# Attention, experts and a dense network on one core: buffers for keys and values, and the load and scatter times of the order

## The chip, the cores and the metric

The kernel runs on one core of a Trainium2 chip. The metric is the device time of one execution in microseconds (us), the median of several executions; smaller is better. Five engines work side by side, each in the order of its own instruction list: PE (TensorE, matrix products; its weight loads are a row of their own, PEld), DVE (VectorE), ACT (ScalarE), POOL (GpSimd) and SP (SyncE, which here only issues transfers and reads registers).

## The reference

Three stages follow one another on float32 data:

```python
def sm_attn(qq, kk, vv):
    s = scale * np.matmul(qq, kk.transpose(0, 1, 3, 2))
    s = s - np.max(s, axis=-1, keepdims=True)
    a = np.exp(s)
    a = a / (np.sum(a, axis=-1, keepdims=True) + 1e-09)
    return np.matmul(a, vv)
p_packed = sm_attn(p, k, v)          # 32 queries per head over 576 keys
out = sm_attn(q, p_packed, p_packed) # 576 queries per head over 32 keys
```

q, k and v are 8 x 8 x 576 x 64 (batch, head, position, width), p is 8 x 8 x 32 x 64. The output, as 4608 tokens of width 512, goes to a mixture of 8 experts: each token goes to the one expert with the largest logit (`x @ w_gate` plus a bias by modality), which computes `gate * (relu(x @ w1[e]) @ w2[e])` with a hidden width of 1024. The last stage is a dense network, `g(x @ w_in) @ w_out` with `g(h) = h * sigmoid(1.702 h)` and a hidden width of 2048; its weights come as float64.

## The kernel before

The attention works in eight units: a unit is a pair of batches and one half of the heads (4), and two units make a pair of batches complete. `loads` (lines 236 to 250) brings in the keys, queries and values of a unit, 1.2 MB each, in two transfers per tensor, which SP issues. `stage1` turns the keys with the identity into the tile kT (L447 on PE, L227 or L228 for the copy out), computes the scores (L293), their maxima and exponentials, turns these (L343), and multiplies them with the values (L366). `qT` turns the queries, and `stage2` computes the second attention: scores (L498), subtraction of the maximum, exponential, sum, a normalization on POOL (L526), its turning (L543) and the products (L564). `store` (L580) writes 1152 KB of tokens to a table xs in memory.

When both units of a pair are done, `route` (L590 ff.) picks each token's expert and its place in that expert's list, and POOL writes the list with nine scatters (`send`, L187), 128 tokens each. Three early slots of an expert's work, then a fourth, begin before the attention has ended: `expert` reads registers, `whole_gather` (L1269 ff.) reads a piece of the list on SP (tok<-lst, L1278) and gathers the tokens with POOL (L1281); L1115 and L1423 are the two products of an expert. Then come the remaining slots, and the dense network by blocks of 512 tokens (L1115 and L1545), behind whose start the 32 weight transfers of L1216 and L1221 are taken apart and split by DVE and ACT.

No engine's order is written by hand. Every piece of work is handed to a planner (`Sched`) with an engine, an assumed duration, the tiles that it writes and reads, and a priority. `run` keeps one clock per engine. Again and again it takes the piece that can start earliest (by priority, where several can), and writes its instructions into the program at that place. A piece can start when its engine is free, when everything that it depends on has ended and a latency has passed, and when a buffer for each of its tiles is free; a tile of n buffers may be made again when the tile n places before has been read by all its readers. The latency behind a load is LAT["sp"], unless the piece names its own; the latency behind one of the nine scatters is SEND, and the list read depends on all scatters of its pair of batches. A piece may also have a due time (`after=`) before which the plan doesn't start it: `expert` gives its register reads the due times 110.0, 150.0, 189.9 and 229.9 us of the plan's clock (T - 30000 ns). These numbers make the order only; on the chip each instruction starts when its engine reaches it and what it waits for is done. The chip's waits follow the order in which the program was written: a list read waits for all scatters written before it, and a scatter written behind a list read waits for that read.

The planned duration of an attention load on SP is 3500 ns, of a scatter on POOL 1270 ns, of one register read 550 ns, of an expert's weight load 1500 ns. The loads of the dense network's weights name their own latency (2200).

Of the kernel before, what the change touches and what calls it, by code (L numbers as in the profile page):

```python
# [50 lines left out]
class Sched:  # L51

    LAT = {"pe": 250.0, "sp": 2200.0, "pq": 2200.0}

    def __init__(self):
        self.made, self.given, self.held, self.ops = {}, {}, {}, []
# [5 lines left out]
    def add(self, eng, dur, fn, w=(), r=(), hold=(), prio=0.0, lat=None, deps=(), after=0.0, alts=None):  # L64
# [3 lines left out]
        o.alts = alts or {eng: (dur, fn)}  # L68
        o.lat = self.LAT.get(eng, 170.0) if lat is None else lat
        o.deps = list(deps)  # L70
# [122 lines left out]
def attention(tc, ctx, pctx, c, S, ins, xs, lst, early, scatter_key):  # L193
# [7 lines left out]
    q, k, v, p = ins["q"], ins["k"], ins["v"], ins["p"]  # L201
# [4 lines left out]
    def sb(tag, shape, n=2, dtype=F32):  # L206
        def make():
            serial[0] += 1
            return pw.tile(shape, dtype, tag=tag, name=f"{tag}_{serial[0]}", bufs=n)

        return S.buf(tag, make, n)
# [24 lines left out]
    def loads(u, prio):  # L236
        bp, hg = units[u]
        s = st[u]
        hs = slice(4 * hg, 4 * hg + 4)
        for n, src, bufs, by in (("k", k, 1, 0 if u else -1000), ("q", q, 2, 200), ("v", v, 2, 400)):  # L240
            b = s[n] = sb(n, [P, 4, S0], bufs)

            def load(b=b, src=src):
                for bl in range(2):
                    x = src[2 * bp + bl, hs].rearrange("h s d -> h (s d)")
                    nc.sync.dma_start(
                        b.t[:, 2 * bl : 2 * bl + 2],
                        x.rearrange("(g x) (p y) -> (x p) g y", x=2, p=64),
                    )

            S.add("sp", 3500, load, w=[b], prio=prio + by)
# [338 lines left out]
    def route(bp, L, xr, prio):  # L590
# [72 lines left out]
        def send(j):  # L663
            scatter(
                tc,
                scatter_key,
                c,
                lst,
                bass.IndirectOffsetOnAxis(ap=idx.t[:, j : j + 1], axis=0),
                c["ids"][:, bp, j],  # L670
                None,
            )

        for j in range(n):
            c["sends"].append(
                S.add("pool", 1270, lambda j=j: send(j), r=[idx], prio=prio + j, lat=SEND)
            )
# [36 lines left out]
    for u in range(len(units)):  # L714
        loads(u, (u - 2) * CYC)
# [11 lines left out]


CYC = 1000.0
SEND = 4500.0  # L730

WIDE_UNITS = 6

# [1011 lines left out]
```

## Time and profile before

| | |
|---|---|
| median of 3 executions | 1467.85 us (1465.35 to 1472.35) |
| the profiled execution | 1466.42 us |
| its span, from the first to the last instruction | 1464.6 us |
| PE busy | 1389.6 us, 95% |
| DVE, ACT, POOL busy | 727.6, 499.5, 227.8 us |
| mean granted clock of TensorE | 0.976 |
| moved | 142.64 MB, mean 97 GB/s |

The span is that of one execution taken by the hardware profiler. Busy time counts an engine's instructions; in the rows below, what stands in brackets behind an arrow is how long the engine had been idle before the instruction and what ended that. "issue" there means that the engine waited for nothing that the profile shows. L12 is line 12 of the kernel. The granted clock is the share of full speed that TensorE was given. The trace of SP and of POOL's transfers shows when a transfer was issued, not when it landed.

### The profile page before, as it was taken

How to read it: one execution, taken by the hardware profiler on the slowest of the kernel's cores; microseconds unless marked ns; L12 is line 12 of the kernel's file. 1: busy time of each engine (PE TensorE's matmuls, PEld its weight loads, DVE VectorE, ACT ScalarE, POOL GpSimd, SP SyncE). 2: the span in 40 equal slices, each digit the busy share in tenths (PEclk: the TensorE clock that was granted, in tenths of full speed). 3: DMA queues.
4: the chain of work that ended last, by engine and by line, in shares of the span. 5: the costliest groups of instructions: out<-in, count | busy, mean ns of one | idle time of the engine just before them, and what ended most of it. 6: DMA issues, size and time to landing. Idle time of an engine off the chain costs nothing.

```text
span 1464.6 us, 21602 instructions
## 1 busy us (share of the span) xinstructions
PE 1389.6 (95%) x8444; PEld 1154.4 (79%) x8444; DVE 727.6 (50%) x1425; ACT 499.5 (34%) x937; POOL 227.8 (16%) x301
## 2 busy tenths in 40 slices
PE   6886879998999999999989999999999999999997
PEld 5774557887888888888868888888888888888885
DVE  5675545543687878877773332423224242322222
ACT  3554433443344444433232222323223232322221
POOL 0133250410344333100010010100001010010101
PEclk9998889999999999999999999999999999999999
DMA  8866513744466665643131020201002010000000
GB/s 280 249 192 186 175 40 110 160 143 142 142 192 189 190 198 175 203 142 113 64 109 58 3 70 0 72 1 44 29 0 73 0 58 1 0 29 1 30 0 29
DMA packets 128144, 142.64 MB, mean 97 GB/s; under 512 B 29504, under 2 KB 92992, under 8 KB 128032
## 3 DMA queue, kind: packets, MB, share of 16 engines
q1 hardware_dynamic: 113184, 121.86, 27.3%
q0 software_dynamic: 14848, 19.30, 4.5%
q8 instruction: 68, 1.11, 0.3%
q14 instruction: 44, 0.36, 0.1%
HBM read 112.24 MB, written 28.87 MB: 96 GB/s over the span
## 4 chain that ended last, share of the span: by engine, by line
PE 49%; issue 18%; POOL 3%; DVE 2%; DMA 2%; POOLq 0%; ACT 0%; DVEq 0%; SPq 0%; ACTq 0%
PE b_f L1115 25%; PE o L1545 21%; PE o L1423 4%; POOL nat L1348 3%; DMA nat<-xs,si 1%; POOL out L187 0%; DMA raw<-moe_w_in 0%; DVE two L1370 0%; DVE war L1196 0%; DVE wbr L1196 0%; DMA out<-raw,tok 0%; DVE g L1412 0%; DVE xT L1379 0%; DVE raw L1573 0%; DVE t L1246 0%
## 5 line engine op out<-in xcount | busy, mean ns | idle before, releaser
L1115 PE MATMUL b_f<-xT,wac 128*128 128x512 f32 x1404 | 339.6, 391 | 4.5 <-ACT xT L1500 3.6
L1545 PE MATMUL o<-wbc,g 128*128 128x512 f32 x1404 | 337.6, 389 | 1.3 <-DVE raw L1573 0.8
L1115 PEld LDWEIGHTS b_f<-xT,wac 128*128 128x128 f32 x1404 | 265.2, 189 | 60.6 <-ACT xT L1500 4.0
L1115 PE MATMUL b_f<-xT,war 128*128 128x470 f32 (+1 forms) x1284 | 301.3, 383 | 9.0 <-DVEq L1633 6.3
L1545 PEld LDWEIGHTS o<-wbc,g 128*128 128x128 f32 x1404 | 263.3, 188 | 57.0 <-DVE raw L1573 1.2
L1535 DVE SCALAR_TENSOR_TENSOR two<-two,b_f 128x512 f32<-128x512 f32 x144 | 98.9, 687 | 372.8 <-ACT two L1532 372.6
L1115 PEld LDWEIGHTS b_f<-xT,war 128*128 128x128 f32 x1284 | 242.5, 190 | 48.9 <-issue 7.4
L1532 ACT ACTIVATE two<-b_f 128x512 f32<-128x512 f32 x144 | 86.1, 598 | 413.0 <-PE b_f L1115 413.0
L1423 PE MATMUL o<-g,wbr 128*128 128x470 f32 x960 | 222.5, 379 | 1.6 <-DVE g L1412 1.6
L1423 PEld LDWEIGHTS o<-g,wbr 128*128 128x128 f32 x960 | 181.0, 190 | 27.2 <-DVE g L1412 2.4
L187 POOL DMA_INDIRECT out<-raw,tok x36 | 37.7, 1048 | 821.1 <-ACT raw L1575 814.7
L1541 DVE TENSOR_TENSOR g<-two,g 128x512 fp32r<-128x512 f32 x141 | 97.5, 692 | 81.5 <-ACT g L1538 81.1
L1538 ACT CAST g<-two 128x512 fp32r<-128x512 f32 x141 | 87.5, 621 | 112.2 <-DVE two L1535 103.9
L1348 POOL DMA_INDIRECT nat<-xs,si x90 | 93.4, 1038 | 173.8 <-DVE two L1370 94.8
L1409 ACT ACTIVATE g<-b_f 128x470 fp32r<-128x470 f32 x80 | 45.1, 564 | 121.2 <-PE b_f L1115 118.6
L1190 ACT CAST wbr<-raw 128x512 fp32r<-128x512 f32 x80 | 49.6, 620 | 69.2 <-PE o L1423 63.8
L1412 DVE SCALAR_TENSOR_TENSOR g<-b_f,g 128x470 fp32r<-128x470 f32 x80 | 51.4, 643 | 43.2 <-ACT g L1409 43.2
L1545 PE MATMUL o<-wbr,g 128*128 128x512 f32 x288 | 69.5, 390 | 0.0
L1196 DVE TENSOR_TENSOR wbr<-raw,wbr 128x512 fp32r<-128x512 f32 x80 | 55.8, 698 | 21.7 <-ACT wbr L1190 21.5
L1196 DVE TENSOR_TENSOR war<-raw,war 128x512 fp32r<-128x512 f32 x80 | 55.4, 692 | 16.3 <-ACT war L1190 11.6
L1545 PEld LDWEIGHTS o<-wbr,g 128*128 128x128 f32 x288 | 53.9, 188 | 11.9 <-DVE g L1541 0.4
L1190 ACT CAST war<-raw 128x512 fp32r<-128x512 f32 x80 | 49.3, 616 | 20.0 <-DMA raw<-moe_w 17.0
(211 smaller groups left out, 1089.2 us busy)
## 6 DMA issues: line engine op xcount, KB each, us to landing
raw<-moe_w SPq DMA_DIRECT2D x160, 256.0 KB, 3.4
yT<-two SPq DMA_DIRECT2D x40, 235.0 KB, 3.7
k<-k SPq DMA_DIRECT2D x16, 576.0 KB, 5.3
q<-q SPq DMA_DIRECT2D x16, 576.0 KB
v<-v SPq DMA_DIRECT2D x16, 576.0 KB, 9.4
xs<-xr SPq DMA_DIRECT2D x8, 1152.0 KB, 5.9
nat<-yT SPq DMA_DIRECT2D x9, 1024.0 KB
raw<-moe_w_in SPq DMA_DIRECT2D x16, 512.0 KB, 4.5
```

Of the source, the lines that this page charges most:

```text
L1115: nc.tensor.matmul(h.t[:, 0:n], wa[:, a, kc], x[kc].t[:, b, 0:n], start=(kc == 0 and i == 0), stop=(kc == 3 and i == 2),)
L1190: nc.scalar.copy(d, src(i))
L1196: nc.vector.tensor_tensor(d, src(i), h.bitcast(F32), ALU.subtract)
L1348: nc.gpsimd.indirect_dma_start(self.rows(xg)[:, b], None, xs, bass.IndirectOffsetOnAxis(ap=idx.t[:, b : b + 1], axis=0))
L1409: nc.scalar.activation(g.t[:, 0, 0:W], h.t[:, 0:W], AF.Relu)
L1412: nc.vector.scalar_tensor_tensor(g.t[:, 1, 0:W], h.t[:, 0:W], 0.0, g.t[:, 0, 0:W].bitcast(F32), ALU.max, ALU.subtract,)
L1423: nc.tensor.matmul(os[d].t[:, 0:W], w.t[1][:, a, d * P : (d + 1) * P], g.t[:, b, 0:W], start=(fc == 0 and m == 0), stop=(fc == NC1 - 1 and ...
L1532: nc.scalar.activation(th.t, h.t, AF.Tanh, scale=0.851)
L1535: nc.vector.scalar_tensor_tensor(th.t, th.t, 1.0, h.t, ALU.add, ALU.mult)
L1538: nc.scalar.copy(g.t[:, 0], th.t)
L1541: nc.vector.tensor_tensor(g.t[:, 1], th.t, g.t[:, 0].bitcast(F32), ALU.subtract)
L1545: nc.tensor.matmul(os[k].t, g.t[:, a, k * P : (k + 1) * P], w.t[1][:, b], start=(i == 0 and m == 0), stop=(i == n - 1 and m == 2),)
```

## The change

Three numbers that the planner uses are changed, and the numbers of buffers of two tiles are exchanged. No instruction is added or removed. The planner assumes 4500 instead of 2200 ns from the end of a load's issue to the start of its readers (all loads of both plans that don't name a latency of their own: the attention's, the list reads and the experts' weights) and 8000 instead of 4500 ns behind a scatter of the lists. A key tile has two buffers instead of one, and a value tile one instead of two; all are of 9216 bytes per partition, so the memory used is the same.

```diff
-    LAT = {"pe": 250.0, "sp": 2200.0, "pq": 2200.0}
+    LAT = {"pe": 250.0, "sp": 4500.0, "pq": 2200.0}
...
-        for n, src, bufs, by in (("k", k, 1, 0 if u else -1000), ("q", q, 2, 200), ("v", v, 2, 400)):
+        for n, src, bufs, by in (("k", k, 2, 0 if u else -1000), ("q", q, 2, 200), ("v", v, 1, 400)):
...
 CYC = 1000.0
-SEND = 4500.0
+SEND = 8000.0
```

## Rows read from the trace of the kernel before

**Rows 1.** The page: PE's busy time (share) and instructions, and its 40 slices.

```profile
PE 1389.6 (95%) x8444; PEld 1154.4 (79%) x8444; DVE 727.6 (50%) x1425; ACT 499.5 (34%) x937; POOL 227.8 (16%) x301
...
PE   6886879998999999999989999999999999999997
```

**Rows 2.** Table by stage: stretch, its length, busy time (instructions) by engine, granted clock, DMA.

```profile
0.00:280.00 280.00, 229.91 (x3247) 178.19 (x3248) 161.30 (x519) 121.67 (x285) 83.95 (x134) 0.91 0.60 172
280.00:1465.00 1185.00, 1159.64 (x5199) 976.25 (x5197) 566.26 (x906) 377.87 (x652) 143.82 (x168) 0.99 0.26 80
120.00:160.00 40.00, 25.27 (x357) 16.49 (x353) 21.55 (x74) 14.47 (x35) 19.02 (x24) 0.76 0.67 173
160.00:196.00 36.00, 29.80 (x497) 23.94 (x481) 23.50 (x80) 18.89 (x41) 3.59 (x6) 0.93 0.44 138
210.00:220.00 10.00, 9.64 (x58) 5.70 (x59) 2.82 (x9) 4.36 (x12) 8.27 (x7) 0.70 0.19 27
```

**Rows 3.** Waits of PE, 0 to 280 us: total, times, longest.

```profile
PE b L366 <- issue: 12.5, 8, 3.7
PE b L543 <- POOL A L526: 10.2, 2, 5.1
PE b L447 <- DMA k<-k: 8.8, 3, 5.0
```

**Rows 4.** POOL in order of time: start, duration, instruction [idle before].

```profile
133.09 0.97 POOL L187 DMA_INDIRECT lst<-ids,idx  x1 [0.19 <-issue]
...
144.34 0.97 POOL L187 DMA_INDIRECT lst<-ids,idx  x1 [10.17 <-DMA tok<-lst]
...
190.23 1.02 POOL L187 DMA_INDIRECT lst<-ids,idx  x1 [13.01 <-DVE cs L656]
...
199.31 0.98 POOL L187 DMA_INDIRECT lst<-ids,idx  x1 [7.94 <-DMA tok<-lst]
```

**Rows 5.** SP in order of time: transfers at their issue.

```profile
122.37 0.89 SPq L246 DMA_DIRECT2D k<-k  x2
...
140.91 0.32 SPq L1278 DMA_DIRECT2D tok<-lst  x1
...
194.40 0.30 SPq L1278 DMA_DIRECT2D tok<-lst  x1
```

**Rows 6.** PE in order of time: ends of waits, and products with the values (L366).

```profile
74.49 0.46 PE L366 MATMUL b<-v,e1T 64*32 64x64 f32 x32 [1.10 <-issue]
...
85.08 1.24 PE L366 MATMUL b<-v,e1T 64*32 64x64 f32 x81
...
88.94 1.65 PE L366 MATMUL b<-v,e1T 64*32 64x64 f32 x55 [0.63 <-issue]
...
108.27 1.66 PE L366 MATMUL b<-v,e1T 64*32 64x64 f32 x144
...
133.39 0.69 PE L447 MATMUL b<-ident,k 128*128 128x128 f32 x2 [2.93 <-DMA k<-k]
...
146.45 1.11 PE L543 MATMUL b<-ident,A 128*128 128x128 f32 x4 [5.08 <-POOL A L526]
...
210.36 1.11 PE L543 MATMUL b<-ident,A 128*128 128x128 f32 x4 [5.11 <-POOL A L526]
```

**Rows 7.** Waits of PE, 280 us to the end: the longest.

```profile
PE b_f L1115 <- DVEq L1633: 6.3, 1, 6.3
```

**Rows 8.** Waits in SP's queue, 0 to 300 us: total, times, longest.

```profile
SPq L246 <- PE b L447: 54.7, 10, 12.4
...
SPq L580 <- DVE xr L228: 30.0, 7, 13.5
...
SPq L246 <- PE b L366: 12.7, 3, 4.9
```

**Rows 9.** Transfers of the tile k, then of v: issue to landing, one half-load.

```profile
DMA to landing us min/median/max: 4.4/5.3/10.5
...
DMA to landing us min/median/max: 7.7/9.4/11.2
```

## The prediction

> **What bounds the kernel now.** I read the page's busy line and its 40 slices first [rows 1]: TensorE (PE) is busy 95% of the span, and from about the eighth slice on its digit is 9 almost everywhere. What is not 9 lies in the first seven slices, the attention. The table by stage says it in microseconds [rows 2]: of the first 280 us PE is busy 229.9, so 50.1 us are idle, and the mean granted clock there is 0.91; of the 1185 us behind it only 25.4 us are idle at 0.99. An edit of the attention's order can therefore win at most those 50.1 us and some of the lost clock; behind 280 us it can mainly lose.
>
> Next, the waits of PE in the first 280 us [rows 3], because they say what these 50 us are. Three kinds matter here. 12.5 us are gaps inside the product of scores and values (L366) with no releaser: nothing in the change speaks to them. 10.2 us are two waits of 5.1 us for POOL's normalization (L526). 8.8 us are three waits for a key load; 5.0 us of them are the first load of all, which nothing can hide. So loads hold PE up only a little (3.8 us behind the first), and the two waits for POOL are the largest thing that an order can cure.
>
> Then the engines behind the two POOL waits [rows 4, 5, 6]. Of the nine scatters of the second pair of batches the eighth is issued at 133.09, and the ninth only at 144.34, after 10.17 us of waiting for the list read (tok<-lst). That read itself stands in SP's queue until 140.91: it reads the list which the eight scatters before it write, and waits for the eighth to land. Behind the ninth scatter stands the normalization that PE wants: PE resumes at 146.45 after 5.08 us. The same happens with the third pair: first scatter at 190.23, list read at 194.40, the second scatter at 199.31 after 7.94 us, the other seven behind it at 1.28 us each, then the normalization, PE idle until 210.36 (5.11 us). The stall is thus made by where the order puts the list read among nine scatters: in between, it costs; ahead of all or behind all, POOL doesn't stop. So it is with these two of the four list reads.
>
> **The change part by part.** The sum is made against the profiled execution, 1466.42 us (span 1464.6 and 1.8 around it). The median is 1467.85, 1.4 above; I add that at the end.
>
> *Longer time for loads (2200 to 4500).* No instruction is added; a load's consumers are planned 2.3 us later, and the emitted order changes. Two steps follow. First, the whole planned attention starts 2.3 us later, since the first transposes wait for the first key load [rows 3]. Second, the early experts' list reads do not move with it: their planning is held by fixed due times (the after= of expert, 110.0 and 150.0 us, plus two or three register loads of 0.55 each, so 111.1 and 151.6 us in the plan's clock). So each list read slides forward by 2.3 us against the scatters, which the plan spaces at 1.27 us. The read at 194.40 stands behind one scatter: it is ahead of all nine if the shift is more than something between 0 and 1.27 us, which 2.3 us is. The read at 140.91 stands behind eight: it needs 8.9 to 10.2 us, which a 2.3 us shift doesn't give; it would come behind the fifth or sixth, and the ninth scatter would end when it does now, because the wait for landing and the read (7.8 us from 133.09 to 140.91, then 3.4 to 144.34) is only put in another place of the same row. So of two stalls I take one: -5.1 us. Bounds: 0 to -10.2.
>
> With the stall goes what it does to the clock: in the 10 us behind it PE is busy 9.64 us at a granted clock of 0.70 [rows 2], part of the time at the lower of the two levels (1.2 instead of 2.4 GHz). 9.64 x 0.30 = 2.9 us of that work is lost. I take all of it, since PE did nothing before the fall but wait for POOL: -2.9 us, bounds 0 and -2.9.
>
> The same shift starts the expert work that fills PE's holes 2.3 us earlier; between 160 and 196 us PE is idle 6.2 of 36 us [rows 2], 17%, so -0.4 us (0 to -0.9).
>
> In the experts and the dense layers behind 280 us the weight loads are planned at 1.5 + 4.5 instead of 1.5 + 2.2 us. On the chip PE hardly waits there: the longest wait in 1185 us is 6.3 us, at the branch of the program [rows 7], and 25.4 us is all its idle time [rows 2]. A worse order on VectorE could show here: I take 0, bounds -1 and +3.
>
> *Longer time for scatters (4500 to 8000).* It matters only where a list read becomes due within 8.0 us of the last scatter that it needs. The last scatter of the second pair starts at 144.34, and the read it serves is issued at 194.40, 50 us later [rows 4, 5]. The fixed due time decides, not the scatter: 0, with bounds 0 and 0 as long as the plan's distance is above a sixth of the chip's.
>
> *Two buffers for keys.* SP's waits show what it removes [rows 8]: 54.7 us in ten waits for the key transposes (L447), which must end before the next key load may be issued. But SP waiting is not PE waiting. The one place where PE then waits is the load issued at 122.37: its transposes resume at 133.39 after 2.93 us [rows 5, 6]. With a second buffer that load could be issued a whole unit earlier. Where does the stall go? PE comes 2.93 us sooner to the wait at 146.45, which POOL ends, not PE: while the first POOL stall stays, the gain is 0. If it goes, it is -2.9. I take 0. In the first units PE waits for no other key load but the first, so an earlier one there is worth 0.
>
> *One buffer for values.* This adds a wait: the load of unit u+1 may be issued only when the product (L366) of unit u is done; before, unit u+2 waited so (12.7 us in three waits [rows 8]). A value load takes 7.7 to 11.2 us to land, median 9.4 [rows 9], and its second half is issued about 0.5 us behind the first, so 10 us. From the end of one unit's product to the start of the next there are 17.7 us or more, as from 90.59 to 108.27, with one exception: from 74.95 to 85.08 [rows 6], 10.1 us. There the load comes out between 1.9 us early and 1.6 us late: I take +0.5, bounds 0 and +2. Queued behind such a load on SP are the next unit's query and key loads, and then the store of the output; with two key buffers they have a unit's time to spare.
>
> A rule of the Trainium skill speaks against the longer load time: "DMA: Bandwidth & Descriptors", section "Anatomy of one DMA", gives a transfer about 2.0 us plus its bytes over 436 GB/s, by which one half of a key load (590 KB) would take an estimated 3.4 us, and the old planned time was already ample. The trace doesn't agree: key halves took 4.4 to 10.5 us, median 5.3, value halves 9.4 [rows 9].
>
> *Sum of the likeliest case:* 1466.4 - 5.1 - 2.9 - 0.4 + 0.5 = 1458.5; plus 1.4 gives **1460 us**, its own range 1454 to 1466.
>
> **The rivals.** *Both stalls go* (the planned attention shifts by more than 9 us, or the first read falls behind all nine scatters): a further 5.1, the key wait of 2.9, and the clock of 120 to 160 us (25.27 us busy at 0.76: 6.1 us). 1460 - 14 = 1446. For it: a single step of -1.3 us is enough to free the first read at its rear. Against: the load time pushes the other way.
>
> *Nothing comes of it*: the shift is eaten by other changes of order, a list read still stands among scatters in both places, or POOL's stall gives way to another wait of the same size. 12.5 us of PE's gaps have no releaser at all [rows 3], and an order can meet more of them. 1468, range 1463 to 1473.
>
> *Slower through the single value buffer*: SP works its queue in order. If a store that waits for the last rows of the output (up to 13.5 us [rows 8]) stands in front of a value load, this comes 13.5 + 10 - 17.7 = 5.8 us late where the products are 17.7 us apart, and 13.4 late where they are 10.1 apart. One of each is 19 us; three quarters of it, since not all of PE's other work stands behind the product, give 1482, from 1474 up. It decides only where the store's wait lasts beyond 7.7 us. Against: the planner knows of the buffer and puts loads by when they may start.
>
> *Slower through needless waiting*: if loads land as early as the rule above says, the longer time only puts work off, in the plan 2.3 us at each of seven further units; half of it, 8 us, on PE's path gives 1476. The 5.3 to 9.4 us that loads took speak against it.
>
> **How the numbers follow.** Chances: likeliest case 0.42, both stalls 0.14, nothing 0.24, value buffer 0.15, needless waiting 0.05. About 0.5% (7.3 us) is what a measurement of this kernel can tell from no change. Under 1460.5 lie some 0.26 of the likeliest case, all 0.14 of the second and 0.04 of the third: faster 0.44. The rest of these two cases but 0.03 is within: 0.16 + 0.17 and 0.01 from the last: same 0.34. Slower 0.22. The range, 1445 to 1480, leaves out the better half of the second case and the worse half of the fourth.
>
> **What would show it.** In the changed kernel's trace the second list read should stand ahead of all nine scatters of its pair, POOL's scatters there should run at 1.28 us without a gap, and PE's wait near 210 us should be gone; a wait for POOL near 140 us should remain; key loads should be issued one unit earlier, and PE should wait for none but the first; value loads should follow each L366. The prediction is wrong if both reads stay among scatters, if PE waits for a value load, or if PE's idle time behind 280 us grows beyond 28 us.

## The result and the profile after

The changed kernel takes 1446.24 us (median of four executions, 1444.27 to 1449.59), the kernel before beside it 1466.6 (four, 1461.32 to 1472.35): a ratio of 0.9863, with an interval of 0.982 to 0.9906. That is 20.4 us less, where the forecast had 1460, 7.9 less than the median of before known to it. The profiled execution took 1447.34 us with a span of 1445.6, 19.0 under the span of before.

Busy line and slices of the page, changed kernel (before: [rows 1]):

```profile
PE 1382.7 (96%) x8444; PEld 1151.3 (80%) x8444; DVE 729.4 (50%) x1420; ACT 501.1 (35%) x942; POOL 228.0 (16%) x301
...
PE   6988979998999999999989999999999999999997
```

PE's idle time fell from 75.0 to 62.9 us (span less busy), which is 12.1 of the 19.0; the other 6.9 are busy time, the same 8444 products at a granted clock of 0.979 instead of 0.976 over the span. The table by stage, changed kernel (before: [rows 2]; stretch, length, busy by engine with instructions, granted clock, DMA share, GB/s):

```profile
0.00:280.00 280.00, 242.00 (x3333) 190.52 (x3334) 168.98 (x526) 129.75 (x302) 87.05 (x135) 0.93 0.64 186
280.00:1445.60 1165.60, 1140.71 (x5113) 960.78 (x5111) 560.39 (x895) 371.37 (x640) 140.95 (x166) 0.99 0.25 78
```

Behind 280 us the idle time is what it was, 24.9 against 25.4 us. Everything lies in the attention: 38.0 us idle there instead of 50.1.

To see where, I cut both traces at the first scatter of each pair of batches, since the scatters come in the same order in every kernel here. Before, these stand at 77.9, 124.13, 190.23 and 259.35 us; in the changed kernel at 78.6, 127.44, 176.48 and 237.94. The stretch from pair two to pair three fell by 17.1 us, the one behind it by 7.7; the others grew by 0.7, 2.6 and 2.4. These lengths don't hold the same work: into each of the two stretches that fell 21 products fewer fall (730 and 709, 544 and 523 in the rows), and more into the others. So PE's idle time in a stretch says more than its length. The two stretches in the kernel before, in the same columns:

```profile
124.13:190.23 66.10, 47.20 (x730) 34.18 (x723) 36.96 (x119) 27.81 (x65) 21.47 (x28) 0.82 0.59 162
190.23:259.35 69.12, 59.65 (x544) 44.10 (x543) 33.81 (x102) 26.27 (x58) 21.69 (x28) 0.90 0.29 76
```

and in the changed one:

```profile
127.44:176.48 49.04, 41.51 (x709) 30.90 (x706) 34.52 (x108) 26.15 (x64) 22.52 (x29) 0.90 0.70 191
176.48:237.94 61.46, 52.95 (x523) 39.62 (x523) 31.49 (x97) 24.80 (x56) 21.95 (x29) 0.92 0.29 81
```

In the first of them PE idles 7.5 us instead of 18.9, and its clock is 0.90 instead of 0.82. In the second the idle time hardly moved (8.5 against 9.5); it is shorter because 21 products fewer fall into it. So the question is what took 11.4 us of idle time out of pair two's stretch. POOL in order of time, changed kernel (before: [rows 4]):

```profile
127.44 1.01 POOL L187 DMA_INDIRECT lst<-ids,idx  x1 [13.36 <-DVE p_m L913]
...
138.25 0.96 POOL L187 DMA_INDIRECT lst<-ids,idx  x1 [0.33 <-DMA lst<-ids,idx]
139.22 2.06 POOL L526 TENSOR_TENSOR A<-A,mx 128x512 f32<-128x512 f32 x2
...
176.48 1.02 POOL L187 DMA_INDIRECT lst<-ids,idx  x1 [13.02 <-DVE cs L656]
185.49 0.98 POOL L187 DMA_INDIRECT lst<-ids,idx  x1 [7.87 <-DMA tok<-lst]
```

The nine scatters of pair two now run from 127.44 to 139.2 without the gap of 10.17 us. Pair three still has its gap, 7.87 us. SP's transfers say why (before: [rows 5]):

```profile
83.47 1.87 SPq L246 DMA_DIRECT2D k<-k  x2
...
113.66 1.00 SPq L246 DMA_DIRECT2D k<-k  x2
...
120.10 0.52 SPq L580 DMA_DIRECT2D xs<-xr  x1
123.45 0.33 SPq L1278 DMA_DIRECT2D tok<-lst  x1
123.98 1.77 SPq L1166 DMA_DIRECT2D raw<-moe_w  x1
...
127.26 0.90 SPq L246 DMA_DIRECT2D q<-q  x2
...
171.13 0.57 SPq L580 DMA_DIRECT2D xs<-xr  x1
180.50 0.31 SPq L1278 DMA_DIRECT2D tok<-lst  x1
```

The first list read is issued at 123.45, ahead of all nine scatters; before, it stood behind eight. The second one comes at 180.50, still behind one. It follows the store of the output (xs) as it did before, 184.88 then 194.40. With two key buffers the key load that was issued at 122.37, the seventh, leaves at 83.47, and the last at 113.66. The order around the first list read is another too: before, the last query load stood ahead of the read and the last key load behind it, and in the changed kernel it is the other way round. Before:

```profile
128.28 0.88 SPq L246 DMA_DIRECT2D q<-q  x2
...
143.56 0.90 SPq L246 DMA_DIRECT2D k<-k  x2
```

PE's waits follow, changed kernel, 0 to 280 us (before: [rows 3]), and the two places where it waited for POOL (before: [rows 6]):

```profile
PE b L343 <- ACT e L317: 7.6, 3, 3.4
PE b L366 <- issue: 6.3, 4, 3.1
PE b L543 <- POOL A L526: 6.1, 3, 5.3
PE b L447 <- DMA k<-k: 5.7, 2, 4.8
```

```profile
140.34 0.66 PE L543 MATMUL b<-ident,A 128*128 128x128 f32 x4 [0.41 <-POOL A L526]
...
196.51 1.11 PE L543 MATMUL b<-ident,A 128*128 128x128 f32 x4 [5.31 <-POOL A L526]
```

One stall of 5.1 us is gone, and the key wait of 2.93 us with it. New is a wait of 7.6 us in three for the exponentials (L317), where the trace of before has 0.9: part of the gain is given back there. It comes with the buffers, which alone have 7.0 us of it. In SP's queue the value loads now wait for the product L366 (before: [rows 8]), and PE's waits name no value load:

```profile
SPq L246 <- PE b L366: 35.9, 7, 10.0
SPq L246 <- PE b L447: 22.3, 7, 7.0
```

### The profile page after: what moved, and what is told of

It reads as the page before. It is cut to its first block, busy times and chain, and to the rows that moved or that the text cites. A ratio compares the mean times of both kernels' runs of the same rounds, so it can differ in the third digit from the quotient of the medians.

```text
span 1445.6 us, 21604 instructions
## 1 busy us (share of the span) xinstructions
PE 1382.7 (96%) x8444; PEld 1151.3 (80%) x8444; DVE 729.4 (50%) x1420; ACT 501.1 (35%) x942; POOL 228.0 (16%) x301
## 4 chain that ended last, share of the span: by engine, by line
PE 56%; issue 17%; POOL 1%; DMA 1%; DVE 0%; POOLq 0%; DVEq 0%
PE b_f L1115 28%; PE o L1545 21%; PE o L1423 7%; POOL nat L1348 1%; POOL out L187 0%; DMA raw<-moe_w_out 0%; DMA nat<-xs,si 0%; DMA out<-raw,tok 0%; DVE raw L1573 0%; DVE g L1541 0%; POOLq L1740 0%; DVE war L1196 0%; DVE two L1370 0%; POOL tick L186 0%; DVE wbr L1196 0%
## 5 line engine op out<-in xcount | busy, mean ns | idle before, releaser
L1115 PEld LDWEIGHTS b_f<-xT,wac 128*128 128x128 f32 x1404 | 265.1, 189 | 60.4 <-ACT xT L1500 4.4
L1190 ACT CAST wbr<-raw 128x512 fp32r<-128x512 f32 x80 | 49.7, 621 | 59.8 <-PE o L1423 58.5
L1196 DVE TENSOR_TENSOR wbr<-raw,wbr 128x512 fp32r<-128x512 f32 x80 | 55.8, 698 | 18.9 <-ACT wbr L1190 18.5
L1196 DVE TENSOR_TENSOR war<-raw,war 128x512 fp32r<-128x512 f32 x80 | 56.8, 711 | 15.2 <-ACT war L1190 10.2
L1190 ACT CAST war<-raw 128x512 fp32r<-128x512 f32 x80 | 49.3, 616 | 12.5 <-DMA raw<-moe_w 10.2
```

What stands on the lines that cost most here:

```text
L1115: nc.tensor.matmul(h.t[:, 0:n], wa[:, a, kc], x[kc].t[:, b, 0:n], start=(kc == 0 and i == 0), stop=(kc == 3 and i == 2),)
L1190: nc.scalar.copy(d, src(i))
L1196: nc.vector.tensor_tensor(d, src(i), h.bitcast(F32), ALU.subtract)
```

## The experiments

All ratios are to the kernel before on the same chip, with a 95% interval. The runs fell on three chips; single profiled executions are compared by their stretches between the scatters. In the table, p2 to p3 is the time from the first scatter of pair two to that of pair three, with PE's products and idle time in it, and p3 to p4 is the next; the times are us. The changed kernel was profiled three times: p2 to p3 took 49.0, 51.0 and 45.3 us, p3 to p4 61.5, 62.5 and 61.3, so a few microseconds in the first of them are spread. "Waits for weights" are those of ACT's casts at L1190 (into war and wbr) for an early expert's weights, 100 to 200 us.

| kernel | ratio | p2 to p3 | products | PE idle | p3 to p4 | first read stands | waits for weights |
|---|---|---|---|---|---|---|---|
| before | 1 | 66.1 | 730 | 18.9 | 69.1 | behind 8 | 11.8 |
| load time alone | 0.9911 | 59.1 | 686 | 15.2 | 65.3 | behind 3 | 1.3 |
| buffers alone | 0.9963 | 59.9 | 729 | 17.6 | 62.3 | behind 4 | 14.4 |
| weights' load time alone | 0.9958 | 62.4 | 663 | 18.7 | 64.0 | behind 8 | 5.5 |
| changed, first read behind one | 0.9917 | 55.1 | 723 | 12.8 | 61.8 | behind 1 | 7.5 |
| changed | 0.9863 | 49.0 | 709 | 7.5 | 61.5 | ahead | 1.8 |
| changed, second read ahead too | 0.981 | 46.1 | 709 | 6.3 | 53.9 | ahead | 2.3 |

**Which part does it.** Two kernels take one part of the change alone.

```diff
-    LAT = {"pe": 250.0, "sp": 2200.0, "pq": 2200.0}
+    LAT = {"pe": 250.0, "sp": 4500.0, "pq": 2200.0}
```

> The kernel before with the longer load time alone (4500). Its first list read stands behind three of the nine scatters of its pair, the second behind one. Theory A (what counts is where the list reads stand): both POOL stalls of about 5 us remain, and the time is that of before within 0.5%, 1460 to 1473 us. Theory L (the load time itself, readers placed when loads really land, is the gain): 1446 to 1452. Theory B (the buffers are the gain): 1466.

Measured: 0.9911 (0.9881 to 0.9941), 1449.0 us against 1461.2.

```diff
-        for n, src, bufs, by in (("k", k, 1, 0 if u else -1000), ("q", q, 2, 200), ("v", v, 2, 400)):
+        for n, src, bufs, by in (("k", k, 2, 0 if u else -1000), ("q", q, 2, 200), ("v", v, 1, 400)):
```

> The kernel before with two key buffers and one value buffer alone. Its first list read stands behind four of nine scatters, the second behind one. Theory A (position of the reads): the stalls remain; the key wait of 2.9 us goes but lies in front of the first stall: 1459 to 1470 us, at most 0.5% faster. Theory B (the buffers are the gain, through the key wait and the key turnings that follow it): 1446 to 1452. Theory L: 1466.

Measured: 0.9963 (0.9944 to 0.9982), 1456.8 us. The first time is the one that theory L gave; the second lies between those of theory A and theory B, and neither gave it. Both parts gain, and 0.9911 x 0.9963 = 0.9874 is the whole within its interval. But neither frees a list read: in order of time, the load time alone on POOL, then PE with the buffers alone:

```profile
132.35 0.97 POOL L187 DMA_INDIRECT lst<-ids,idx  x1 [8.80 <-DMA tok<-lst]
```

```profile
145.28 1.12 PE L543 MATMUL b<-ident,A 128*128 128x128 f32 x4 [7.91 <-POOL A L526]
```

With the load time alone POOL still stops for 8.80 us in pair two and for 7.39 in pair three, and yet 12 us are gained. So the reads' places can't be the whole matter. With the buffers alone the key wait is gone, and the wait for POOL behind it has grown from 5.08 to 7.91 us: by 2.83 us, about what the key wait was (2.93). So far that is as the prediction had it, and yet 4 us are gained.

The longer scatter time needed no run: the kernel with SEND alone has the same instruction lists as the kernel before on all five engines, and the changed kernel with SEND at 4500 the same as the changed one.

**The first read's place.** The due time of one read is moved by 0.1 us, so that it falls behind the first scatter, with everything else as in the changed kernel:

```diff
-    def expert(self, i, prio, deps=()):
+    def expert(self, i, prio, deps=(), due=None):
...
-            self.S.add("sp", 550, lambda m=m: load(m), prio=prio + n, lat=0, after=prio, deps=deps)
+            self.S.add("sp", 550, lambda m=m: load(m), prio=prio + n, lat=0, after=prio if due is None else due, deps=deps)
...
-        e = F.expert(-k, T - 30000, deps=[chosen])
+        e = F.expert(-k, T - 30000, deps=[chosen], due=T - 29900 if k == 1 else None)
```

> The changed kernel with one edit: the first early slot's register reads are due 0.1 us later in the plan. Every engine's instruction list stays the same; only the first list read now comes behind the first of the nine scatters instead of ahead of it, so that it waits for that scatter's landing, and the second scatter waits for the read. Theory A: the stall of POOL (8 to 10 us) and PE's wait behind it come back, 5 us of idle time and up to 6 us of clock: 1451 to 1457 us. Theories B and L: no change, 1446.

Measured: 0.9917 (0.9889 to 0.9945), 1450.0 us, 1 us under the range of theory A. The stretch p2 to p3 takes 55.1 us, where the three traces of the changed kernel have 45.3 to 51.0: 4 to 10 us for the place of this read; PE idles 12.8 us in it, against 6.4 to 8.5. The ratios give 0.5%, 8 us, though the two kernels did not run side by side. Every engine's own order is the same in the plan, so this is the price of the place alone. The trace shows a way that I had not seen. SP, ACT and PE in order of time:

```profile
132.89 0.33 SPq L1278 DMA_DIRECT2D tok<-lst  x1
133.42 2.02 SPq L1166 DMA_DIRECT2D raw<-moe_w  x1
...
137.84 0.62 ACT L1190 CAST war<-raw 128x512 fp32r<-128x512 f32 x1 [5.01 <-DMA raw<-moe_w]
...
139.21 0.52 ACT L317 ACTIVATE e<-b,sm 128x320 f32<-128x320 f32 x1
...
139.88 2.43 PE L343 MATMUL b<-ident,e 128*128 128x128 f32 x9 [8.54 <-ACT e L317]
```

SP stands before the list read until 132.89, since that read waits for a scatter to land. Behind it in SP's queue are the early expert's weights, issued at 133.42 instead of 123.98. ACT's cast of these weights waits 5.01 us, and behind the cast in ACT's order stand the exponentials that PE wants: PE waits 8.54 us. POOL's own stall (9.66 us here) costs PE only 2.5 us in this stretch. So a list read among scatters holds PE up over two ways: over POOL to the normalization, and over SP and ACT to the exponentials.

**The price of one stall.** The second read is put ahead of its scatters, first in the changed kernel, then in the kernel before. Here and below the diff shows the due time alone; the argument `due` is that of the edit above.

```diff
+        e = F.expert(-k, T - 30000, deps=[chosen], due=T - 35000 if k == 2 else None)
```

> The changed kernel with one edit: the second early slot's register reads are due 5 us earlier in the plan, which puts the second list read ahead of all nine scatters of its pair; it stood behind the first. Theory A: POOL's stall of 7.9 us and PE's wait of 5.3 us near 196 us go, and with them some lost clock: 1438 to 1442 us. Theories B and L: 1446. A rival to A, that expert work which fills PE takes the place of the stall anyway: 1444 to 1446.

Measured: 0.981 (0.9782 to 0.9838), 1434.05 us, 4 us under the range of theory A. On a further chip the same kernel and the changed one ran side by side:

> The changed kernel on the same chip as the three kernels beside it. 0.983 to 0.990 where the chip is like the first one; 0.997 was measured on a chip on which PE had further gaps without a releaser behind the attention.

> The changed kernel with the second list read ahead of all nine scatters of its pair, on the same chip as the changed kernel: 7 us less than that (0.995 of it), by theory A's price of one POOL stall of 5.3 us and its clock.

Measured: 0.9866 (0.9828 to 0.9904), 1441.3 us, and 0.9807 (0.9764 to 0.9849), 1434.6: 6.7 us less. The changed kernel's result is repeated by the first. From pair three to pair four, first the changed kernel and then with the second read ahead:

```profile
173.96:235.26 61.30, 51.80 (x523) 38.59 (x523) 31.51 (x97) 24.75 (x56) 21.93 (x28) 0.94 0.30 82
```

```profile
171.70:225.46 53.76, 49.47 (x523) 37.24 (x523) 31.55 (x97) 24.82 (x56) 21.93 (x29) 1.00 0.33 93
```

The same 523 products take 7.5 us less: 5.2 of it idle time, 2.3 busy time at a clock of 1.00 instead of 0.94. This version is faster than both kernels of the case.

```diff
+        e = F.expert(-k, T - 30000, deps=[chosen], due=T - (30000 if k == 1 else 36000) if k < 3 else None)
```

> The kernel before with the second list read alone put ahead of all nine scatters of its pair (its register reads due 6 us earlier in the plan; buffers and load time as before, every scatter at the same place of the plan). This is the term that the prediction priced at 5.1 us of idle time and 2.9 us of clock. Theory A (reads): 8 us less, ratio 0.9945, within 0.992 and 0.997. Rival, that POOL's stall gives way to another wait: 0.998 to 1.0.

Measured in the kernel before: 0.9952 (0.9916 to 0.9988), 1499.9 us against 1507.8 on that chip; p3 to p4 is 60.4 us. In the plan the order of PE, ACT, DVE and POOL is that of the kernel before. The stall's price of 8.0 us in the prediction (5.1 + 2.9) stands against 6.7 us by the times in the changed kernel, and in the kernel before 8.0 by the times and 8.7 by the stretch (69.1 less 60.4, from two chips).

**Is the first read alone as good in the kernel before?** Both reads ahead, with the old load time and buffers, and then with the longer load time; beside them the changed kernel:

```diff
+        e = F.expert(-k, T - 30000, deps=[chosen], due=T - (47000 if k == 1 else 40000) if k < 3 else None)
```

> The kernel before with both list reads ahead of the scatters of their pairs (due 17 and 10 us earlier in the plan), buffers and load time as before. If the reads explain the change (A), it is as fast as the changed kernel with its second read ahead: ratio 0.978 to 0.985. If reads and load order add up (A and L each a part), it lacks the part of the load order, some 6 us or more: 0.985 to 0.990. If the load order is all (L): 1.0.

> The longer load time alone, with both list reads ahead of the scatters of their pairs; one key and two value buffers as before. The load time alone gave 0.9911 with both stalls in place. If reads and load time add up: 0.978 to 0.983. If the load time's gain was itself a matter of the stalls: as before with both reads ahead, 0.985 to 0.990.

> The changed kernel once more, on the same chip as the three kernels beside it, as their measure. 0.9863 of before was measured; 0.983 to 0.990 here.

Measured: 0.9963 (0.9925 to 1.0002), 0.9997 (0.9962 to 1.0033) and 0.9971 (0.9935 to 1.0008). None is clear of no change. Of the first, theory L had that; of the two others it wasn't expected, and on this chip, where the kernel before takes 1507.8 us, it holds of the changed kernel too. Its stretch p2 to p3 is 51.0 us there, against 65.7 in the kernel before with the second read ahead; the gain is lost outside this stretch. The changed kernel from 260 to 700 us, and PE's waits there:

```profile
260.00:700.00 440.00, 407.58 (x1827) 351.18 (x1828) 282.48 (x474) 173.23 (x318) 105.02 (x99) 0.95 0.52 157
```

```profile
PE b_f L1115 <- issue: 15.4, 13, 5.9
PE o L1423 <- ACT g L1409: 11.9, 3, 5.9
```

PE idles 32.4 us in these 440, about half of it in gaps without a releaser, where on the first chip it idles 7.4 and the kernel before 10.5. The other three kernels traced on this chip idle 28.7 to 40.4 us there, so it isn't the change that does it. Why this chip does so stays open. I take from it the stretches, and of the ratios only that of the second read alone, whose interval is clear of 1. With both reads ahead in the kernel before, p2 to p3 is still 64.6 us (65.7 with only the second ahead, on this chip). PE's waits in that stretch, and POOL around its scatters:

```profile
PE b L564 <- ACT e L317: 8.0, 1, 8.0
PE b L447 <- DMA k<-k: 5.8, 2, 3.9
PE b L447 <- ACT kT L227: 5.6, 1, 5.6
```

```profile
127.00 1.69 POOL L1281 DMA_INDIRECT nat<-xs,tok  x1 [9.30 <-DMA tok<-lst]
...
140.38 0.97 POOL L187 DMA_INDIRECT lst<-ids,idx  x1 [1.94 <-DMA nat<-xs,tok]
```

The long gap between the scatters is gone, and other waits stand in its place: for the single key buffer, for the copy of its transposes, and for the exponentials. PE idles 22.9 us in the stretch, against 19.0 with only the second read ahead. ACT's waits for weights are 15.1 us there. With the longer load time too the stretch is 59.8. So this edit gains 1 us in the stretch, not 8. But it isn't the first read alone that it moves: with the read 17 us earlier two gathers come ahead of the first scatter, and the plan's order changes on PE, ACT and DVE too. What the read alone is worth in the kernel before isn't shown.

**The casts of the weights.** The kernel before, with the longer time for the experts' weight loads alone, so that the plan puts their casts later. The attention's order on SP and POOL is left as it is; on PE, ACT and DVE it isn't, and eight of the attention's copies move from DVE to ACT:

```diff
-        S.add("sp", 1500, load, w=[raw], prio=prio, deps=ereg)
+        S.add("sp", 1500, load, w=[raw], prio=prio, deps=ereg, lat=4500.0)
```

> The kernel before with the longer load time (4500) for the experts' weight loads alone; attention loads, list reads and buffers as before, and both list reads behind as many scatters as before (eight and one). Theory C: the gain of the longer load time alone (0.9911) lay in ACT's queue, where the first weight casts (L1190) stand in front of the attention's exponentials and wait for loads that SP is late to issue, 11.8 us between 100 and 200 us; planned 2.3 us later they let the exponentials pass. By C that wait falls under 5 us and the ratio is 0.990 to 0.996. By theory L in its first form (attention loads planned as late as they land): 1.0, and ACT's wait stays near 10 us.

Measured: 0.9958 (0.9937 to 0.9978), 1455.3 us against 1462.5. Waits of ACT for the early weights, 100 to 200 us: before, with this edit, and in the changed kernel:

```profile
ACT war L1190 <- DMA raw<-moe_w: 10.4, 2, 6.9
ACT wbr L1190 <- DMA raw<-moe_w: 1.4, 2, 1.2
```

```profile
ACT war L1190 <- DMA raw<-moe_w: 5.5, 1, 5.5
```

```profile
ACT war L1190 <- DMA raw<-moe_w: 1.8, 1, 1.8
```

6 to 7 us are gained with both of POOL's stalls in place and the first read still behind eight scatters (PE waits 10.1 us for POOL in the first 280 us, 10.2 before), about half of what the longer load time gains alone. ACT's wait is halved, to 5.5 us where theory C wanted under 5. But PE's idle time in that stretch is what it was:

```profile
121.50:183.93 62.43, 43.71 (x663) 30.88 (x656) 34.00 (x111) 29.40 (x70) 21.14 (x28) 0.84 0.61 172
```

That is 18.7 us, 18.9 before. The stretch is 3.7 us shorter because 67 products fewer fall into it, 3.5 us of busy time; the wait for POOL grew from 5.1 to 6.0 us. PE's idle time falls elsewhere, by 2.9 us from pair three to pair four. So the weights' load time gains, but that it does so by ACT's casts isn't shown. The last kernel has the buffers and both reads ahead, but the old load time:

```diff
+        e = F.expert(-k, T - 30000, deps=[chosen], due=T - (52000 if k == 1 else 40000) if k < 3 else None)
```

> Two key buffers and one value buffer, the old load time, and both list reads ahead of the scatters of their pairs (the first by a hair, the second by 9 us in the plan). Three waits in a row were found between the second and the third pair of batches: key load, list read, weight casts. If each is enough to hold this stretch by itself (C): no key wait, no POOL stall, and since SP is not held, little waiting of ACT, so this stretch takes 46 to 52 us instead of 60, and the ratio is 0.978 to 0.986. If the longer load time has a part of its own: 54 us or more, and 0.987 to 0.992.

Measured: 0.9919 (0.9892 to 0.9946), 1451.1 us; p2 to p3 is 53.2 us. Theory C had 0.978 to 0.986, and fails. The time is 16.5 us above the changed kernel with both reads ahead on the same chip, so the longer load time has a share that is neither the buffers nor the reads. It isn't ACT's wait for weights either: from 100 to 200 us this kernel has none. Of the 17.3 us between the spans of the two profiled executions 7.2 are idle time of PE, and 10.0 busy time at a granted clock of 0.977 instead of 0.990. Which waits make this share stays open.

## Why the prediction came out as it did

The time lies in the range, by 1.2 us at its lower end, and 8 us under the likeliest case's own range (1454 to 1466). That it is inside is luck: the sum of that case was 7.9 us, and the one stall that it took away went in the other pair of batches. Of the signs that the prediction named, the four on the list reads and POOL came out the other way round; those on the key and value loads held, but for 0.9 us of a second wait for keys.

*What bounds the kernel:* right. The gain lies in the first 280 us, half of it and more in idle time, the rest in the clock that came back with it.

*Longer load time, the reads:* this step failed. It had the second read slide ahead and the first stay; it was the other way round. I took both reads to be held by their due times, and in the kernel before neither is. The second is held by SP's queue, behind the store of the output, and moves with the attention, so a shift of the whole attention does nothing to it. The first was held there too, by the query load that was issued at 128.28. In the plan it stood at 114.3 us; with either part of the change SP is free when it is due, and it stands at 111.1. The first scatter of its pair, planned at 105.3 us before, comes at 107.6 with the load time alone, at 106.8 with the buffers alone, and at 111.1 with both, just behind the read. So it takes load time and buffers together, as the two parts alone show (behind three and behind four scatters), and a margin so small that 0.1 us of plan time undoes it. The price of one stall, 8.0 us, was right in size.

*Two key buffers, 0:* the condition was right and the size was not. With POOL's stall in place the key wait of 2.9 us does go into POOL's wait, as the buffers alone show. But they gain 4 us all the same, so that something else than this wait gains by them; what, isn't shown.

*What stands behind the list read:* this term was missing. I followed the read to POOL alone and did not ask what is queued behind it on SP, or behind the casts on ACT, though the casts' waits of 11.8 us were in the trace of before. With the first read behind one scatter PE waits 8.5 us by this way and 2.5 by POOL. How much of the 20 us it is isn't shown.

*What the load time does besides:* the largest term that was missing. It was priced by the reads alone, and it gains 12 us with both stalls in place. No run says by which wait.

*One value buffer, +0.5:* right within its bounds; loads wait for L366, and PE waits for none of them. *Scatter time, 0* and *behind 280 us, 0:* right. *12.5 us of gaps in L366, "nothing in the change speaks to them":* they are 6.3, 10.6 and 7.1 us in the three profiles of the changed kernel, and 5.2 where the buffers alone are changed. No run takes them by themselves, so whether the change does something to them is open.

*The rivals:* the time is that of "both stalls go", 1446, but not its mechanism: only one went, and the other 6.7 us were still to be had, as the kernel with both shows on the same chip. "POOL's stall gives way to another wait" is what the kernel before with both reads ahead does. "Needless waiting" did not come: the longer load time gains alone. The rule of the Trainium skill behind it ("DMA: Bandwidth & Descriptors", "Anatomy of one DMA") is given there for transfers that GpSimd issues. The key loads here are issued by SP. The key wait and the read stand in a row in pair two's stretch, and taking one away lengthens the other, as the buffers alone show; the change takes away both.

## What to carry to other kernels

When a wait on one engine is to go, list what stands behind the waiting instruction on every in-order queue that it blocks, SP's loads and ACT's casts too; a transfer that one engine issues late may reach the bounding engine over a second one. Where several waits stand in a row in one stretch, price them together, since an experiment that takes one away can show little. Before a read is said to be held by its due time, look at what is issued just ahead of it. And where a stretch of two kernels is compared, count the products in it, since a planner moves work from one stretch to another.

## What was not expected of the hardware

A small list read between scatters of the same table costs POOL 7.2 to 10.4 us in every trace here that has one, though the read's issue takes 0.3 us: about 4 to 8 us until the last scatter before it has let it go, and some 3.4 to 5.0 until the scatter behind it starts. And one chip ran the kernel before in 1507.8 us where two others took 1461 to 1463, with the gaps shown above from 260 to 700 us; a gain of 1.4%, seen twice elsewhere, came out as 0.3% there.
